# Moving the homes of TensorE's operands in SBUF by a few dozen bytes

## The chip, the cores and the metric

The kernel runs on one core of a Trainium2 chip. The metric is the time of one execution on the device in microseconds (us), as the median of several runs.

## What is computed

Attention with two kinds of window feeds a token mixer and a feed-forward block, all in fp32 (B = 8 sequences, H = 8 heads, S = 576, D = 64; model width 512, inner width 2048):

```python
scores = where(mask, q @ k.T / sqrt(64), -1e9)     # heads 0-3: band of 32; heads 4-7: every 4th of 128
x = softmax(scores) @ v                            # heads side by side: [8, 576, 512]
mixed = real(fft(fft(x, axis=1), axis=2))
u = x + mixed
un = (u - mean(u)) / sqrt(var(u) + 1e-6)           # over the 512 channels
out = u + maximum(un @ w_ch1, 0) @ w_ch2           # 512 -> 2048 -> 512
```

`w_ch1` and `w_ch2` arrive as 64-bit floats and are turned into fp32 on the chip.

## The kernel before

Each operation is handed to a planner (`Plan`) with its engine, an estimated cost, a priority and the buffers that it reads and writes. The planner simulates the engines and writes out one order of instructions per engine. Buffers with a tag share a fixed number of slots (`ut` 4, `h` 6, `row` 2); a tile's place in SBUF comes from the pool that it is taken from.

The work has three parts. Attention and the mix (Fourier transforms as matmuls against the tables `seq`, `chn`, `tail_sb`, `alt_sb`) run sequence by sequence in the first part. In the gaps, and behind them, the **filling stage** takes pairs of token tiles through the first NF1 = 5 of 16 slices of the inner width: `up` (L926) multiplies tokens `ut` by `wa1`, the relu's output goes to `h`, `down` (L942) multiplies `h` by `wa2`, and the sum over these five slices is put away in memory. The **second stage** takes 9 chunks of 512 tokens (4 token tiles of 128) through the other 11 slices: `product` (L1199) multiplies blocks of the first weight by `xb`, the tokens of the chunk in 7 combinations, and `down` (L942) the relu's output by `wd` and `wa2`. A chunk has passes p = 0 to 5. A pass of two slices has 7 products of 6 matmuls (42) and up to 8 downs of 3 matmuls (24, for the slices of the pass before); pass 5 has one slice and 24 product matmuls. Its blocks come from `ups`:

```python
ups = [
    [block(pair0, i) for i in range(7)],
    [block(pair1, i) for i in range(7)],
    [block(pair2, i) for i in range(5)] + [block(more, i) for i in range(2)],
    [block(tail_w, i) for i in range(4)] + [spare_up(i) for i in range(3)],   # spare_up: in wa1
    [spare_up(3 + i) for i in range(7)],
    [block(tail_w, 4 + i) for i in range(3)],
]
```

Every product in fp32r is three matmuls, high and low halves: (high, high), (low, high), (high, low). The two halves of a buffer lie whole multiples of 512 bytes apart, and so do the slices that a matmul takes. All of these matmuls load a new stationary operand of 128 columns. The moving operand has 256 columns in `up` and `product`, 512 in `down`. In `up` and `product` the weight is stationary and the tokens move; in `down` `h` is stationary and the weight moves.

SBUF is filled from two sides. On the left lie, in this order, the pool `ffn` (tags `ut`, `h`, `row`), `const` (`flip_sb`, `wa1`, `wa2`) and then `mix`, which `second()` closes and replaces by `pair1`, `more`, `wd2` to `wd5`, `xb` and the buffers `s1` to `c22`. On the right lies `att`, which `first()` closes and replaces by `pair0`, `wd0`, `wd1`, `pair2` and the staging buffers, these later by `tail_w` (`third()`). [...] The start of each buffer in a partition, modulo 128, is in the program:

| buffer | start modulo 128, before |
|---|---|
| `ut`, `h`, `row` | 0 |
| `wa1`, `wa2`, `pair1`, `more`, `wd2` to `wd5`, `xb` | 32 |
| `pair0`, `wd0`, `wd1`, `pair2`, `tail_w` | 96 |
| `tq`, `kb`, `pm`, `perm_sb` (attention) | 64 |
| `ident_sb`, `ptsb` | 32 |

In what follows, two operands of a matmul are called n apart when their starts modulo 128 differ by n, counted the shorter way.

Of the kernel before, what the change touches and what calls it, by code (L numbers as in the profile page):

```python
# [9 lines left out]
F32 = mybir.dt.float32  # L10
F32R = mybir.dt.float32r
I32 = mybir.dt.int32
# [7 lines left out]
P = 128  # L20
# [5 lines left out]
TOK1 = 2 * P  # L26
# [6 lines left out]
NH = 6  # L33
# [144 lines left out]
class Plan:  # L178
# [20 lines left out]
    def add(self, eng, cost, fn, r=(), w=(), prio=0.0, nbytes=0, at=0.0):  # L199
        op = Op()  # L200
        op.eng, op.cost, op.fn, op.prio, op.nbytes = eng, cost, fn, prio, nbytes
        op.num, op.after, op.ready, op.start = len(self.ops), [], at, None
        self.ops.append(op)
        deps, bufs = set(), {}
        for items, writes in ((r, False), (w, True)):
            for it in items:
                b, key = it if isinstance(it, tuple) else (it, None)
                bufs[id(b)] = b
                keys = set(b.writer) | set(b.readers) if key is None else {key, None}
                for x in keys:  # L210
                    if x in b.writer:
                        deps.add(b.writer[x])
                    if writes:
                        deps.update(b.readers.get(x, ()))
        for items, writes in ((r, False), (w, True)):
            for it in items:
                b, key = it if isinstance(it, tuple) else (it, None)
                if writes:
                    if key is None:
                        b.writer, b.readers = {None: op.num}, {}  # L220
                    else:
                        b.writer[key] = op.num
                        b.readers.pop(key, None)
                else:
                    b.readers.setdefault(key, []).append(op.num)
        op.bufs = list(bufs.values())
        for b in op.bufs:
            b.left += 1
        deps.discard(op.num)
        op.waits = len(deps)  # L230
        for d in deps:
            self.ops[d].after.append(op)
        return op
# [134 lines left out]
def fused_kernel(ctx: ExitStack, tc, q, k, v, w1, w2, seq, tail, chn, alt, mask, ident, perm, flip, out):  # L368
    nc = tc.nc
    plan = Plan()  # L370
# [11 lines left out]

    pools = {}
    pools["psum"] = ctx.enter_context(tc.tile_pool(name="psum", bufs=1, space=bass.MemoryType.PSUM))
    pools["ffn"] = ctx.enter_context(tc.tile_pool(name="ffn", bufs=1))
    const = ctx.enter_context(tc.tile_pool(name="const", bufs=1))
    mix_ctx, att_ctx, stage_ctx = ExitStack(), ExitStack(), ExitStack()
    pools["mix"] = keep = mix_ctx.enter_context(tc.tile_pool(name="mix", bufs=1))
    pools["att"] = heads = att_ctx.enter_context(tc.tile_pool(name="att", bufs=1, side="right"))

# [3 lines left out]
    def bank(tag):  # L394
        return plan.buf(lambda: pools["psum"], tag, [P, 512], F32, banks[tag])
# [9 lines left out]
    def ffnb(tag, shape, dtype=F32, bufs=2):  # L405
        return plan.buf(lambda: pools["ffn"], tag, shape, dtype, bufs)

    def fixed(pool_, shape, dtype, name):
        b = Buf(ap=pool_.tile(shape, dtype, name=name))
        if pool_ is keep:  # L410
            mixed.add(id(b))
        return b

    def utb(i=0):
        return ffnb("ut", [P, 2, KT, TOK1], F32R, NUT)

    flip_sb = fixed(const, [P, 8], I32, "flip_sb")
    wa1 = [fixed(const, [P, 2, KT, P], F32R, f"wa1_{f}") for f in range(NF1)]
    wa2 = [fixed(const, [P, 2, C], F32R, f"wa2_{f}") for f in range(NF1)]
    mask_sb = fixed(heads, [QB, 3, KB], F32, "mask_sb")  # L420
# [15 lines left out]
    def dma(fn, r, w, prio, nbytes, slow=1):  # L436
        return add("SP", 0.5, fn, r, w, prio, nbytes * slow)
# [3 lines left out]
    def start():  # L441
        dma(lambda: nc.sync.dma_start(out=mask_sb(), in_=mask), (), (mask_sb,), -7.9, QB * 3 * KB * 4)
        dma(lambda: nc.sync.dma_start(out=ident_sb(), in_=ident), (), (ident_sb,), -7.8, P * 3 * P * 4)
        dma(lambda: nc.sync.dma_start(out=perm_sb(), in_=perm), (), (perm_sb,), -7, QB * QB * 12)
        dma(lambda: nc.sync.dma_start(out=flip_sb(), in_=flip), (), (flip_sb,), 50, P * 32)

        def zero(t, eng, cost, fn, key=None, prio=-5.0):
            add(eng, cost, fn, (), ((t, key) if key is not None else t,), prio)

        zero(half, "DVE", 0.07, lambda: nc.vector.memset(half(), -0.5))  # L450
        for n, t in enumerate(kbs):
            for e in range(2):
                def clear(t=t, e=e):
                    ps = slice(64 * e, 64 * e + 64)
                    nc.vector.memset(t()[ps, 1 - e], 0.0)
                    nc.vector.memset(t()[ps, e, 0:WIN], 0.0)
                zero(t, "DVE", 0.8, clear, ("z", e), -6.0 + n)
        for t in xs + xtail:
            zero(t, "DVE", 0.07, lambda t=t: nc.vector.memset(t()[:, C:C + 1], 0.0), "pad")
        def gaps():  # L460
            for r in (32, 96):
                nc.vector.memset(eot().bitcast(F32)[r:r + 32, 0], 0.0)
        zero(eot, "DVE", 0.4, gaps, ("gap", 0))
        zero(eot, "DVE", 0.2, lambda: nc.vector.memset(eot().bitcast(F32)[0:32, 1], 0.0), ("gap", 1))
        zero(ye, "DVE", 0.2, lambda: nc.vector.memset(ye().bitcast(F32), 0.0))
        for b in range(B):
            dma(lambda b=b: nc.sync.dma_start(
                out=xsm[b]()[0:1], in_=kbs[0]()[0:1, 1, WIN:WIN + C],
            ), ((kbs[0], ("z", 0)),), ((xsm[b], "zero"),), 12 * b + 6, 2048)
        for i in range(2):  # L470
            for m in range(2):
                add("POOL", 0.06, lambda i=i, m=m: nc.gpsimd.dma_start(out=seq_sb[i]()[:, m], in_=seq[i, m]),
                    (), ((seq_sb[i], m),), 6 + i, P * 2 * NSP * 4, at=T_SEQ + i)
                add("POOL", 0.06, lambda i=i, m=m: nc.gpsimd.dma_start(out=chn_sb[i]()[:, m], in_=chn[i, m]),
                    (), ((chn_sb[i], m),), 9 + i, P * 2 * NEP * 4, at=T_CHN + i)
        add("POOL", 0.06, lambda: nc.gpsimd.dma_start(out=tail_sb(), in_=tail), (), (tail_sb,), 6.5, P * 3 * NSP * 4, at=T_SEQ + 0.5)
        add("POOL", 0.06, lambda: nc.gpsimd.dma_start(out=alt_sb(), in_=alt), (), (alt_sb,), 8, P * NEP * 4, at=T_SEQ + 4)
# [461 lines left out]
    def down(h, wf, acc, s, first, last, prio):  # L939
        def go():  # L940
            for n, (a, p) in enumerate(PASSES):
                nc.tensor.matmul(  # L942
                    acc(), lhsT=h()[:, a, P * s:P * s + P], rhs=wf()[:, p],
                    start=(first and n == 0), stop=(last and n == 2),
                )
        add("PE", 3 * pe(C), go, (h, wf), (acc,), prio)
# [140 lines left out]
    def fill(ut, tiles, at=None):  # L1087
        prio = P_FILL + (tiles[0] if at is None else at) * P_FILLT
        late = at == NREST - 1 or tiles[0] < NREST <= tiles[0] + 2 * NLATE
        hs = []  # L1090
        for f in range(NF1):
            h = ffnb("h", [P, 2, TOK1], F32R, NH)
            z = bank(("pt", "av")[f % 2] if late else "ff")
            hs.append(up(ut, wa1[f], z, h, prio, TOK1))
        for s, idx in enumerate(tiles):
            acc = bank("sc" if late else "ff")
            for f in range(NF1):
                down(hs[f], wa2[f], acc, s, f == 0, f == NF1 - 1, prio)
            keep_part(idx, acc, prio)
# [20 lines left out]
    def second():  # L1120
        mix_ctx.close()
        pools["wbb"] = left = ctx.enter_context(tc.tile_pool(name="wbb", bufs=1))
        pair1.ap = tile_of(left, 7, "pair1")
        more.ap = tile_of(left, 2, "more")
        for i in range(2, 6):
            wd[i].ap = left.tile([P, 2, C], F32R, name=f"wd{i}")
        xb.ap = left.tile([P, 7, 2, 2, TOK1], F32R, name="xb")

    def third():
# [86 lines left out]
        return s  # L1216

    def put_h(z, need):
        h = ffnb("h", [P, 2, TOK1], F32R, NH)
        add("ACT", act(TOK1), lambda: nc.scalar.activation(  # L1220
            out=h()[:, 0], in_=z(), func=AF.Relu), need, ((h, 0),), SOON)
        add("DVE", dve(TOK1), lambda: nc.vector.scalar_tensor_tensor(
            h()[:, 1], z(), 0.0, h()[:, 0].bitcast(F32), op0=ALU.max, op1=ALU.subtract),
            (*need, (h, 0)), ((h, 1),), SOON)
        return h
# [89 lines left out]
```

## Time and profile before

| | |
|---|---|
| median of 3 runs | 1122.07 us (1121.26 to 1122.24) |
| the profiled execution | 1123.04 us |
| its span, first to last instruction | 1121.3 us |
| mean granted TensorE clock | 0.981 |
| TensorE matmuls busy | 1072.7 us, 96% of the span, 7066 matmuls |
| VectorE busy | 726.6 us, 65% |
| ScalarE busy | 522.5 us, 47% |
| GpSimd busy | 289.4 us, 26% |

"Busy" is the time in which an engine has at least one instruction under way. Matmuls overlap, so their own durations (some 280 ns for 256 columns, 395 ns for 512) are longer than the interval from one start to the next. The chain of work follows the last instruction back to what released it; its pieces join without gaps, so a piece of n matmuls divided by n gives their interval.

### The profile page before, as it was taken

Reading aid. Unit: us, or ns where it says so; the run is one execution under the profiler, and the core shown is the slowest. Engines: PE = TensorE matmul, PEld = TensorE weight load, DVE = VectorE, ACT = ScalarE, POOL = GpSimd, SP = SyncE. Lnnn points to the kernel's source line nnn. Section 1 sums busy time; section 2 is a strip of 40 time slices with the busy share of each in tenths; the row PEclk is TensorE's granted clock in tenths of the full one; section 3 lists DMA queues with packets and bytes.
Section 4 is the critical chain, followed back from the end, with each engine's and each line's share of the span. In section 5 each row is a group of like instructions: output and inputs, shape, how many; then the busy total and the mean of one; then the engine's idle time right before and its main releaser. Section 6 shows DMA issues by size and latency. Waiting matters only on the chain.

```text
span 1121.3 us, 20217 instructions
## 1 busy us (share of the span) xinstructions
PE 1072.7 (96%) x7066; PEld 948.1 (85%) x7066; DVE 726.6 (65%) x2318; ACT 522.5 (47%) x1331; POOL 289.4 (26%) x341
## 2 busy tenths in 40 slices
PE   5799999999999999999989899999999999999997
PEld 3567888889888988899978798898988889888886
DVE  5789988767867778867769763536363545454523
ACT  4587656546555634344435443333333333333331
POOL 2025365343434254300030421121202120212200
PEclk8799999999999999999999899999999999999999
DMA  9677567656655344345423250505050504041211
GB/s 313 175 207 220 159 193 195 193 143 184 176 165 149 115 136 123 110 122 152 129 87 114 66 160 1 150 1 151 1 150 1 142 9 132 20 107 45 93 59 38
DMA packets 104310, 137.05 MB, mean 122 GB/s; under 512 B 9656, under 2 KB 62328, under 8 KB 104208
## 3 DMA queue, kind: packets, MB, share of 16 engines
q1 hardware_dynamic: 100624, 126.85, 39.0%
q0 software_dynamic: 3040, 8.09, 2.4%
q8 instruction: 56, 0.92, 0.3%
q10 hardware_dynamic: 544, 0.82, 0.2%
q14 instruction: 46, 0.38, 0.1%
HBM read 97.92 MB, written 37.80 MB: 121 GB/s over the span
## 4 chain that ended last, share of the span: by engine, by line
PE 81%; DVE 11%; DMA 3%; issue 2%; POOL 1%; ACT 1%; SPq 0%; DVEq 0%; ACTq 0%; POOLq 0%
PE sc L942 15%; PE ff L1199 13%; PE mix L1199 8%; PE ff L926 7%; PE pt L942 6%; PE av L942 6%; PE ff L942 6%; PE sc L513 5%; PE av L547 5%; PE mix L775 2%; PE pt L540 2%; PE mix L729 2%; PE pt L926 2%; DVE pm L521 2%; DMA ut<-in_w_dram 1%
## 5 line engine op out<-in xcount | busy, mean ns | idle before, releaser
L527 ACT ACTIVATE pm<-pm,mx 96x128 f32<-96x128 f32 x384 | 130.3, 394 | 53.6 <-DVE mx L521 49.9
L1215 ACT COPY s<-ff 128x256 f32<-128x256 f32 x135 | 50.2, 373 | 163.9 <-PE ff L1199 163.5
L513 PE MATMUL sc<-kb,tq 128*96 128x256 f32 x384 | 109.4, 405 | 16.2 <-DMA kb<-in_k_dram 8.0
L926 PE MATMUL ff<-ut,wa 128*128 128x256 f32 x780 | 110.0, 291 | 3.3 <-DVE h L934 3.3
L521 DVE CUSTOM_DVE_ANT_0 pm<-sc,mask_sb 96x128 f32<-96x128 f32 x384 | 92.8, 278 | 24.4 <-PE sc L513 23.4
L942 PE MATMUL sc<-wa,h 128*128 128x512 f32 x420 | 106.4, 395 | 0.0
L926 PEld LDWEIGHTS ff<-ut,wa 128*128 128x128 f32 x780 | 99.7, 192 | 5.1 <-DVE h L934 3.9
L942 PE MATMUL ff<-wa,h 128*128 128x512 f32 x390 | 95.8, 397 | 0.0
L547 PEld LDWEIGHTS av<-vt,ptsb 128*96 128x96 f32 x768 | 79.9, 171 | 16.7 <-issue 5.5
L1068 POOL TENSOR_TENSOR ut<-ut 128x512 f32<-128x512 f32 x36 | 50.7, 1428 | 166.5 <-DVE ut L1024 86.4
L547 PE MATMUL av<-vt,ptsb 128*96 128x65 f32 x768 | 84.5, 253 | 6.9 <-DVE xt L559 5.3
L942 PEld LDWEIGHTS sc<-wa,h 128*128 128x128 f32 x420 | 76.2, 188 | 15.6
L942 PEld LDWEIGHTS ff<-wa,h 128*128 128x128 f32 x390 | 71.6, 188 | 15.7
L942 PE MATMUL sc<-wd,h 128*128 128x512 f32 x324 | 84.1, 394 | 0.0
L513 PEld LDWEIGHTS sc<-kb,tq 128*96 128x96 f32 x384 | 57.9, 173 | 30.0 <-issue 13.3
L1246 DVE TENSOR_TENSOR c<-s,s 128x256 f32<-128x256 f32 x45 | 22.3, 496 | 89.6 <-ACT s L1215 86.5
L1199 PEld LDWEIGHTS ff<-xb,pair 128*128 128x128 f32 x540 | 74.0, 189 | 6.6 <-ACT s L1215 0.7
L1024 DVE STREAM_TRANSPOSE ut<-ut 128x512 f32<-128x512 f32 (+1 forms) x76 | 71.7, 984 | 11.0 <-DMA ut<-us 10.9
L1199 PE MATMUL ff<-xb,pair 128*128 128x256 f32 x540 | 76.8, 281 | 0.5 <-ACT s L1215 0.5
L1081 POOL TENSOR_TENSOR xb<-ut,xb 128x512 fp32r<-128x512 f32 x27 | 36.8, 1363 | 133.5 <-ACT xb L1078 133.5
L1220 ACT ACTIVATE h<-row 128x256 fp32r<-128x256 f32 x90 | 37.5, 417 | 64.1 <-DVE row L1236 38.2
L980 POOL DMA_INDIRECT ut<-us,flip_sb x20 | 19.8, 988 | 180.9 <-DMA ut<-us 87.2
(158 smaller groups left out, 2318.4 us busy)
## 6 DMA issues: line engine op xcount, KB each, us to landing
vt<-in_v_dram SPq DMA_DIRECT2D x32, 390.0 KB
ut<-in_w_dram SPq DMA_DIRECT2D x20, 512.0 KB
us<-uc SPq DMA_DIRECT2D x36, 257.0 KB
tq<-in_q_dram SPq DMA_DIRECT2D x32, 288.0 KB
part<-row SPq DMA_DIRECT2D x36, 256.0 KB
ut<-us SPq DMA_DIRECT2D x36, 256.0 KB
ut<-part SPq DMA_DIRECT2D x36, 256.0 KB
kb<-in_k_dram SPq DMA_DIRECT2D x62, 144.0 KB
```

Source lines behind the costliest of these rows:

```text
L513: nc.tensor.matmul(sc()[:QB, 256 * n:256 * n + 256], lhsT=tq()[:, cols], rhs=kb()[:, :, keys], start=True, stop=True,)
L521: nc.vector.tensor_tensor_reduce(pm()[:, i], sc()[:QB, KB * i:KB * i + KB], mask_sb()[:, masks[blocks[i // 2]]], -0.125, 3.0e38, ALU.add, ...
L527: add("ACT", 0.295, lambda i=i: nc.scalar.activation(out=pm()[:, i], in_=pm()[:, i], func=AF.Exp, bias=mx()[:, i:i + 1], scale=-1.0), ((mx ...
L547: add("PE", 0.16, lambda i=i: nc.tensor.matmul(av()[:QB, 65 * i:65 * i + 65], lhsT=pt()[:, i], rhs=vt()[:, i % 2, blocks[i // 2]], start=T ...
L926: nc.tensor.matmul(z()[:, :n_tok], lhsT=wf()[:, a, kk], rhs=ut()[:, p, kk], start=(kk == 0 and n == 0), stop=(kk == KT - 1 and n == 2),)
L942: nc.tensor.matmul(acc(), lhsT=h()[:, a, P * s:P * s + P], rhs=wf()[:, p], start=(first and n == 0), stop=(last and n == 2),)
L1024: nc.vector.transpose(out=o[back], in_=x[:, g])
L1068: add("POOL", pool(C), lambda: nc.gpsimd.tensor_tensor(out=made(i)(), in0=x(), in1=y(), op=ALU.subtract), (*done, *((raw, ("s", j)) for j ...
L1081: add(eng, (pool if eng == "POOL" else dve)(C), lambda j=j, get=get, lo=lo: lo.tensor_tensor(out=xb()[:, j, 1], in0=get(), in1=xb()[:, j, ...
L1199: nc.tensor.matmul(z()[:, lo:lo + TOK1], lhsT=ap()[:, a, kk], rhs=xb()[:, j, p, kk], start=(start and k == 0), stop=(stop and k == 6 * len ...
L1215: add("ACT", act(TOK1), lambda: nc.scalar.copy(out=s(), in_=src()[:, :TOK1]), (src,), (s,), SOON - 1)
L1220: add("ACT", act(TOK1), lambda: nc.scalar.activation(out=h()[:, 0], in_=z(), func=AF.Relu), need, ((h, 0),), SOON)
```

## The change: other homes for buffers

Nothing but the place of tiles in SBUF is changed. `flip_sb` gets a pool of its own at the left edge, 64 bytes wide, so that `ut` and `row` behind it start at 64. `h` leaves the pool `ffn` for a pool `hidden` behind a gap of 64 bytes, and starts at 0, as do `wa1` and `wa2` behind it. On the right, 96 unused bytes bring `pair0`, `wd0`, `wd1`, `pair2` and `tail_w` from 96 to 0. In `second()`, `pair1`, `more` and `wd2` to `wd5` come to lie at 0 by the 96 bytes gained on the left, and 64 unused bytes put `xb` at 64. Everything on the right moves by 96 bytes, attention's buffers too (64 becomes 96), and so does the mix's part of the left (`ident_sb`: 32 becomes 0).

| matmul | stationary, moving before | apart | after | apart |
|---|---|---|---|---|
| `up` | `wa1` 32, `ut` 0 | 32 | 0, 64 | 64 |
| `down` with `wa2`, `wd2` to `wd5` | `h` 0, weight 32 | 32 | 0, 0 | 0 |
| `down` with `wd0`, `wd1` | `h` 0, weight 96 | 32 | 0, 0 | 0 |
| `product` with `pair1`, `more`, `wa1` | 32, `xb` 32 | 0 | 0, 64 | 64 |
| `product` with `pair0`, `pair2`, `tail_w` | 96, `xb` 32 | 64 | 0, 64 | 64 |

```diff
     pools["psum"] = ctx.enter_context(tc.tile_pool(name="psum", bufs=1, space=bass.MemoryType.PSUM))
+    index = ctx.enter_context(tc.tile_pool(name="index", bufs=1))
+    flip_sb = Buf(ap=index.tile([P, 16], I32, name="flip_sb"))
     pools["ffn"] = ctx.enter_context(tc.tile_pool(name="ffn", bufs=1))
+    gap = ctx.enter_context(tc.tile_pool(name="gap", bufs=1))
+    gap.tile([P, 16], F32, name="gap")
+    pools["hidden"] = ctx.enter_context(tc.tile_pool(name="hidden", bufs=1))
     const = ctx.enter_context(tc.tile_pool(name="const", bufs=1))
     mix_ctx, att_ctx, stage_ctx = ExitStack(), ExitStack(), ExitStack()
+    side = ctx.enter_context(tc.tile_pool(name="side", bufs=1, side="right"))
+    side.tile([P, 24], F32, name="side")
...
+    def hidden():
+        return plan.buf(lambda: pools["hidden"], "h", [P, 2, TOK1], F32R, NH)
+
...
-    flip_sb = fixed(const, [P, 8], I32, "flip_sb")
...
-        dma(lambda: nc.sync.dma_start(out=flip_sb(), in_=flip), (), (flip_sb,), 50, P * 32)
+        dma(lambda: nc.sync.dma_start(out=flip_sb()[:, 0:8], in_=flip), (), (flip_sb,), 50, P * 32)
...
-            h = ffnb("h", [P, 2, TOK1], F32R, NH)
+            h = hidden()
...
             wd[i].ap = left.tile([P, 2, C], F32R, name=f"wd{i}")
+        left.tile([P, 16], F32, name="step")
         xb.ap = left.tile([P, 7, 2, 2, TOK1], F32R, name="xb")
...
-        h = ffnb("h", [P, 2, TOK1], F32R, NH)
+        h = hidden()
```

## Rows read from the trace of the kernel before

**Rows 1.** The page: span, busy time of each engine, chain by engine.
```profile
span 1121.3 us, 20217 instructions
...
PE 1072.7 (96%) x7066; PEld 948.1 (85%) x7066; DVE 726.6 (65%) x2318; ACT 522.5 (47%) x1331; POOL 289.4 (26%) x341
...
PE 81%; DVE 11%; DMA 3%; issue 2%; POOL 1%; ACT 1%; SPq 0%; DVEq 0%; ACTq 0%; POOLq 0%
```

**Rows 2.** Waits of TensorE, 585 to 1121 us: total, times, longest.
```profile
PE ff L1199 <- ACT h L1220: 3.0, 1, 3.0
PE ff L1199 <- ACT s L1215: 0.5, 1, 0.5
```

**Rows 3.** Stretches: busy us of each engine, granted clock, DMA share, GB/s.
```profile
300.00:400.00 100.00, 99.98 (x736) 88.83 (x735) 73.21 (x352) 57.90 (x161) 35.91 (x53) 1.00 0.51 148
...
703.00:761.00 58.00, 58.00 (x366) 52.13 (x365) 28.71 (x53) 22.27 (x53) 11.11 (x9) 1.00 0.26 71
```

**Rows 4.** The chain, 540 to 645 us: start, us, what.
```profile
565.37 1.68 DVE xb L1081
567.04 1.68 DVE ut L860
...
625.88 2.00 DVE ut L1024 x2
```

**Rows 5.** The chain, one chunk of the second stage, 703 to 761 us.
```profile
706.92 0.69 PE ff L1199 x6
...
711.85 1.44 PE mix L1199 x12
713.28 1.40 PE sc L942 x6
...
721.72 0.69 PE ff L1199 x6
722.41 1.36 PE mix L1199 x12
...
732.19 0.69 PE ff L1199 x6
...
742.71 0.71 PE ff L1199 x6
743.42 1.44 PE mix L1199 x12
...
753.28 1.41 PE ff L1199 x12
...
756.10 1.37 PE ff L1199 x12
```

**Rows 6.** The chain, filling stage, 464 to 499 us: `down` x30, `up` x60 and x36.
```profile
470.36 7.00 PE ff L942 x30
477.36 7.10 PE ff L926 x60
484.46 6.99 PE ff L942 x30
491.44 4.26 PE ff L926 x36
```

**Rows 7.** Stretches, instructions of L926 alone: busy us of matmuls and loads.
```profile
300.00:400.00 100.00, 26.76 (x180) 23.28 (x180) 1.00 0.51 148
400.00:580.00 180.00, 85.22 (x660) 83.33 (x660) 0.98 0.43 128
```

**Rows 8.** Groups by line and shape: the transposes in attention (busy, mean ns).
```profile
L540 PE MATMUL pt<-ident_sb,pm 96*128 96x96 f32 x192 | 32.1, 260 | 1.0 <-ACT ptsb L543 1.0
...
L540 PE MATMUL pt<-perm_sb,pm 96*128 96x96 f32 x192 | 30.8, 254 | 3.3 <-ACT ptsb L543 2.4 <-ACT pm L527 0.6
```

## Prediction

> **What bounds the kernel now.** I read the page first, then the chain of work, then the waits, then single stretches of the chain. The page's head and shares [rows 1] say that TensorE is busy for 96% of the span and holds 81% of the chain. The reader should see that this leaves little else to gain from, but also that "busy" tells nothing of pace: a matmul that takes longer is just as busy. So the second question is who TensorE waits for. [...] Only around 427 to 464, 556 to 570 and 622 to 636 us does the chain run mostly over VectorE; three of its pieces are shown [rows 4].
>
> The third look is at pace. In the chain, pieces of one line follow each other without a gap, so a piece's time divided by its count is the interval of a matmul. Rows 5 hold pieces of one chunk, all of them the same instruction: 128 stationary columns, 256 moving ones, the same clock. The products with pair1 (711.85) and with wa1 (743.42) take 1.44 us for 12, which is 120.0 ns. Those with pair2 (722.41) and tail_w (753.28, 756.10) take 1.36, 1.41 and 1.37, which is 113.3, 117.5 and 114.2 ns. By homes, the first two weights start 32 bytes past a multiple of 128, and so does xb: the two operands are 0 apart modulo 128. The others start at 96: they are 64 apart from xb. The matmuls of `up` in the filling stage (weights at 32, tokens at 0, so 32 apart) take 7.10 us for 60 and 4.26 for 36, 118.3 ns [rows 6]. `down` streams 512 columns with h at 0 against weights at 32 or 96, 32 apart either way; 30 take 7.00 or 6.99 us [rows 6] and six of the second stage take 1.40 [rows 5], 233 ns in each.
>
> Whole stretches of one chunk confirm it. From the starts at 721.72, 732.19, 742.71 and 753.28 [rows 5], passes p = 2, 3 and 4 take 10.47, 10.52 and 10.57 us for the same 42 products and 24 downs. They hold 12, 18 and 42 products that are 0 apart. So 30 more of these cost 0.10 us, 3.3 ns each.
>
> **The change part by part.** Every instruction, its order, its waits and the DMAs stay: the planner sees the same tags, slots and costs. Homes alone move. Four families of matmuls get another distance between stationary and moving operand.
>
> A. Products with pair1, more and wa1: 0 apart becomes 64 apart. Per chunk these are 42 (p = 1), 12 (p = 2), 18 (p = 3) and 42 (p = 4), 114; in 9 chunks 1026. At 3.3 ns each: 3.4 us saved. The ends come from rows 5: down from 120.0 to 117.5, 2.6 us; down to 113.8 (the mean of 1.36 and 1.37 over 12), 6.4 us. Nothing saved stays as an end too, if the distance is not the cause (below).
>
> B. `up` in the filling stage: 32 apart becomes 64. It has 1080 matmuls, of which 180 and 660 start after 300 us [rows 7], where TensorE sets the pace; the 240 before I count at nothing, since VectorE, ScalarE and DMA share the chain there. 64 apart costs, as the mean of today's mix, 120.0 - 3.3 = 116.7 ns; from 118.3 that is 1.6 ns times 840, 1.4 us saved. Ends: 117.5 ns, 0.7 us; 113.8 ns, 3.8 us.
>
> C. `down`, 1728 matmuls (540 in the filling stage, 1188 behind): 32 apart becomes 0 apart. No row shows 512 moving columns at 0. Nearest from above: 256 columns at 0 take 1.7 ns more than at 32 (120.0 against 118.3); so much on each of 1728 is 2.9 us lost, and if 512 columns cost twice 120.0, 240 ns, the loss is 6.7 ns each, 11.6 us. Nearest from below: twice 113.8 is 227.6, a gain of 5.7 ns each, 9.8 us. I take nothing: against weights at 32 and at 96, on either side of h, `down` shows the same 233 ns, so it is so far the family that homes move least. Both ends stay for the range.
>
> D. Products with pair0, pair2 and tail_w stay 64 apart, at 0 and 64 now and not at 96 and 32. Today 42 of 120 in a chunk run at the short pace (0.69 for 6 at 706.92, 721.72 and 732.19, 1.36 and 1.37 for 12 [rows 5]), the rest near 117.5. I take no change. All long would lose 42 x 9 x 3.7 ns = 1.4 us, all short gain 78 x 9 x 3.7 = 2.6 us.
>
> E. Attention's and the mix's operands move too, but all tiles of the right side move by the same 96 bytes, and those of the left side likewise, so their distances stay, with one exception: the transposes against ident_sb. They average 260 ns at 32 apart, those against perm_sb at 0 apart 254 [rows 8]; 6 ns on 192 is 1.2 us either way, and I take nothing.
>
> F. Writes by DMA and by the other engines go to other homes. DMA engines are 0.26 busy in a chunk and VectorE 28.71 of 58.00 us [rows 3]; that slack is the cover, and from 585 us on TensorE waited for no DMA at all [rows 2]. Without the cover, VectorE's stretch of 622 to 636 us would grow; ten per cent of it is 1.4 us.
>
> What is late next: where TensorE gets ahead, VectorE's two pieces at 565 and 567 us [rows 4] are met sooner, and a part of B can be lost there; B's lower end covers it.
>
> Sum: -3.4 - 1.4 = -4.8 us. The profiled execution took 1123.04 us (span 1121.3 [rows 1]), 0.97 above the median of the runs, 1122.07. It would take 1118.2, and the median becomes 1117.3.
>
> [...] The row shows 120.0 ns at 0 apart and 113.3 to 117.5 at 64 apart for one instruction at one clock [rows 5]. [...]
>
> **The rivals.** *All short.* Products 64 apart run at two paces that persist over a block, 113.8 and 117.5 ns. If aligned homes make the short one the rule, A gives 6.4, B 3.8 and D 2.6 us: 12.8, so 1109.3. For it: a block keeps its pace once it has it (12 in 1.36). Against it: today each chunk shows both, at one and the same distance.
>
> *All long.* The other pace everywhere: A 2.6 and B 0.7 saved, D 1.4 lost: 1.9, so 1120.2, not to be told from no change. For it: 78 of 120 run so today.
>
> *Homes are not the cause.* The weights that run at 120.0 ns also lie in the left part of the memory, as xb does, and the faster ones on the right. Then the region decides, the low bits do nothing, A and B are 0: 1122.1. For it: in this trace the two can't be told apart. Against it: `up` has both operands on the left and runs at 118.3, between the two.
>
> *Slower.* `down` at 0 apart pays as the products do. At 240 ns for 512 columns it loses 11.6 us against the 4.8 saved: +6.8, so 1128.9. It decides from 2.8 ns a matmul on (4.8 us over 1728). For it: 0 is the slowest distance that the rows show. Against it: a weight load is equally long in both families, and `down` runs twice as many moving columns beside it.
>
> **How the numbers follow.** 0.2% of the time, 2.2 us, is about what a measurement of this kernel can tell from no change. Forecast 0.42 (its own range 1113 to 1119.8), all short or a gain in `down` beside it 0.20, all long 0.10, homes not the cause 0.12, slower by `down` 0.16. Faster is the forecast, all short and a little of all long, 0.64; same 0.21; slower 0.15. The range takes the likeliest, the two that end near today, all short down to 1106, and the small losses in `down` up to 1124.5; it leaves out most of the slower case and a tail with `down` at 227.6.
>
> **What would show it.** In a chunk, pass p = 4 should fall from 10.57 towards 10.43 us, and 12 products with wa1 from 1.44 to 1.41 or less. 60 of `up` should fall from 7.10 to about 7.00. Thirty of `down` should stay within 6.95 to 7.05; 7.2 there would mean the slower case, 6.8 a gain that I have not counted. TensorE's granted clock and its waits should stay. The forecast is wrong if pass p = 4 keeps its 10.57 us, or if `down` moves by more than 2 ns.

## The result, and the profile after

The kernel after takes 1113.39 us (median of 6 runs, 1111.84 to 1114.71), the kernel before on the same chip 1122.63 (6 runs, 1121.26 to 1123.67). The ratio is 0.9917, interval 0.9904 to 0.993: 9.2 us faster. The profiled execution took 1114.71 us, 8.33 less than that of before.

The page of after, beside [rows 1]: span, busy time of each engine, chain by engine.

```profile
span 1112.9 us, 20217 instructions
...
PE 1064.3 (96%) x7066; PEld 944.7 (85%) x7066; DVE 726.0 (65%) x2318; ACT 522.2 (47%) x1331; POOL 288.7 (26%) x341
...
PE 80%; DVE 12%; DMA 3%; issue 2%; POOL 1%; ACT 1%; SPq 0%; DVEq 0%; ACTq 0%; POOLq 0%
```

TensorE executes the same 7066 matmuls and is busy 8.4 us less; the span is 8.4 us shorter. VectorE, ScalarE and GpSimd change by 0.7 us at most. The waits of TensorE from 580 us on, beside [rows 2], and two stretches, beside [rows 3]:

```profile
PE ff L1209 <- ACT h L1230: 3.1, 1, 3.1
PE ff L1209 <- ACT s L1225: 0.5, 1, 0.5
```

```profile
300.00:400.00 100.00, 99.98 (x739) 89.16 (x738) 73.51 (x352) 58.97 (x164) 36.25 (x53) 1.00 0.51 146
698.00:756.00 58.00, 58.00 (x368) 52.30 (x368) 28.68 (x53) 22.24 (x53) 11.14 (x9) 1.00 0.28 74
```

The waits are the old ones, within 0.1 us; the granted clock is 1.00 in both stretches, as before; TensorE is idle for 0.02 of these 158 us, before and after. So the gain is in the pace of its matmuls. It shows in the chain. First the filling stage (start, us, what), beside [rows 6]; L951 is `down`, L935 `up`:

```profile
468.68 6.81 PE ff L951 x30
475.50 7.07 PE ff L935 x60
482.56 6.80 PE ff L951 x30
```

Thirty of `down` took 7.00 and 6.99 us and take 6.81 and 6.80: 233 ns became 227. Sixty of `up` went from 7.10 to 7.07, a mere 0.5 ns each. Then a chunk of the second stage, beside [rows 5]; L1209 is `product`:

```profile
706.87 1.36 PE mix L1209 x12
...
716.65 0.69 PE ff L1209 x6
...
727.04 0.72 PE ff L1209 x6
...
737.47 0.71 PE ff L1209 x6
738.18 1.41 PE mix L1209 x12
739.59 1.39 PE sc L951 x6
...
747.97 1.37 PE ff L1209 x12
```

Products with wa1 (738.18) take 1.41 us for 12 where they took 1.44; those with pair1 (706.87), 1.36. The starts 716.65, 727.04, 737.47 and 747.97 give passes p = 2, 3 and 4: 10.39, 10.43 and 10.50 us, before 10.47, 10.52 and 10.57. Six of `down`, however, take 1.39 here (739.59), little less than the 1.40 of before, at the same distance at which thirty in a row of the filling stage went to 227 ns. Over the whole second stage these downs gain more than this one piece shows (a table by family stands below).

Where the time came from can be read off without the chain. The order of the 7066 matmuls is the same in all kernels below, so the start of the n-th, counted from 0, is a waypoint (us from the span's start; the 3600th lies near the end of the filling stage, and from the 4200th to the 7000th TensorE never stops: 445.00 of the 445.00 us from 655 to 1100 are busy, before and after). Starts by the trace:

```
matmul         500th     3600th    4200th    7000th    4200th to 7000th
before         100.47    548.79    655.07    1101.36   446.29
after          101.07    545.91    650.54    1093.19   442.65
```

From the 500th to the 3600th 3.5 us are gained, to the 4200th another 1.6, from there to the 7000th 3.6.

### The profile page after: what moved, and what is told of

It is laid out like the page before. It is cut to its first block, busy times and chain, and to the rows that moved or that the text cites. A ratio compares the mean times of both kernels' runs of the same rounds, so it can differ in the third digit from the quotient of the medians.

```text
span 1112.9 us, 20217 instructions
## 1 busy us (share of the span) xinstructions
PE 1064.3 (96%) x7066; PEld 944.7 (85%) x7066; DVE 726.0 (65%) x2318; ACT 522.2 (47%) x1331; POOL 288.7 (26%) x341
## 4 chain that ended last, share of the span: by engine, by line
PE 80%; DVE 12%; DMA 3%; issue 2%; POOL 1%; ACT 1%; SPq 0%; DVEq 0%; ACTq 0%; POOLq 0%
PE sc L951 14%; PE ff L1209 13%; PE mix L1209 8%; PE ff L951 6%; PE ff L935 6%; PE pt L951 6%; PE av L951 6%; PE sc L522 6%; PE av L556 4%; PE mix L784 2%; PE mix L738 2%; PE pt L549 2%; PE pt L935 2%; DVE pm L530 1%; DMA ut<-in_w_dram 1%
## 5 line engine op out<-in xcount | busy, mean ns | idle before, releaser
L935 PE MATMUL ff<-ut,wa 128*128 128x256 f32 x780 | 109.0, 289 | 3.7 <-DVE h L943 3.6
L951 PE MATMUL sc<-wa,h 128*128 128x512 f32 x420 | 104.4, 391 | 0.0
L935 PEld LDWEIGHTS ff<-ut,wa 128*128 128x128 f32 x780 | 98.7, 192 | 5.7 <-DVE h L943 4.3
L951 PE MATMUL ff<-wa,h 128*128 128x512 f32 x390 | 93.8, 392 | 0.0
L951 PEld LDWEIGHTS sc<-wa,h 128*128 128x128 f32 x420 | 76.0, 188 | 13.8
L951 PE MATMUL sc<-wd,h 128*128 128x512 f32 x324 | 83.7, 393 | 0.0
L951 PEld LDWEIGHTS ff<-wa,h 128*128 128x128 f32 x390 | 71.6, 188 | 13.8
L1209 PEld LDWEIGHTS ff<-xb,pair 128*128 128x128 f32 x540 | 73.8, 188 | 6.4 <-ACT s L1225 0.7
L1209 PE MATMUL ff<-xb,pair 128*128 128x256 f32 x540 | 76.4, 280 | 0.5 <-ACT s L1225 0.5
```

The source lines that it names most:

```text
L935: nc.tensor.matmul(z()[:, :n_tok], lhsT=wf()[:, a, kk], rhs=ut()[:, p, kk], start=(kk == 0 and n == 0), stop=(kk == KT - 1 and n == 2),)
L951: nc.tensor.matmul(acc(), lhsT=h()[:, a, P * s:P * s + P], rhs=wf()[:, p], start=(first and n == 0), stop=(last and n == 2),)
L1209: nc.tensor.matmul(z()[:, lo:lo + TOK1], lhsT=ap()[:, a, kk], rhs=xb()[:, j, p, kk], start=(start and k == 0), stop=(stop and k == 6 * len ...
```

## The experiments

**Homes modulo 256.** The prediction took distances modulo 128. The runs below showed that the period is 256 (e6), so distances are given here as start of the moving minus start of the stationary operand, modulo 256:

| distance modulo 256 of | before | after |
|---|---|---|
| `up` | 224 | 192 |
| `down` with `wa2`, `wd2` to `wd5` | 32 | 0 |
| `down` with `wd0`, `wd1` | 96 | 128 |
| `product` with `wa1`, `pair1`, `more` | 0 | 64 |
| `product` with `pair0`, `pair2`, `tail_w` | 192 | 192 |

**One part alone: e1, e11, e7.** e1 is the kernel before with `h` alone moved, by 32 bytes modulo 256 (part C): `row` and `flip_sb` stand before it and not behind it. `wa2` and `wd2` to `wd5` are then 0 from it, `wd0` and `wd1` 64.

```diff
+    index = ctx.enter_context(tc.tile_pool(name="index", bufs=1))
+    flip_sb = Buf(ap=index.tile([P, 8], I32, name="flip_sb"))
+    pools["hidden"] = ctx.enter_context(tc.tile_pool(name="hidden", bufs=1))
...
-            h = ffnb("h", [P, 2, TOK1], F32R, NH)
+            h = hidden()
```

> The kernel before with h alone moved, from 0 to 32, so that down has its operands 0 apart and all else stays. Theory 1, the distance between the two operands of a matmul modulo 128 sets its pace: thirty downs of the filling stage take 6.8 us in place of 7.0, and the time falls by some 6 us to about 1116.5. Rival, absolute alignment counts (starts at multiples of 64 are read faster): h gets worse, down stays at 233 ns or slower, and the time is 1122.6 or above.

Measured: 1118.04 us, before 1122.56; ratio 0.9959 (0.9943 to 0.9974). The chain of e1 in the filling stage (L947 `down`, L931 `up`):

```profile
465.70 6.83 PE ff L947 x30
472.52 7.10 PE ff L931 x60
```

`down` fell to 227.7 ns, `up` kept its 7.10. Moving one buffer inside the same region does this, and to a start of 32 modulo 128, which is less aligned than the 0 of before. Nor is it the place of `h` as such: in e11 below `h` lies at the very bytes of after, 32 from `wa2`, and thirty take 7.00. Neither the region nor the alignment of an operand is the cause here; the distance of the two is.

e11 gives `up` alone its distance of after, 192 (part B): the weights, `h` and `xb` all move by 128 bytes modulo 256, `ut` by 96, so that all other distances of the table stay.

```diff
+    lead = ctx.enter_context(tc.tile_pool(name="lead", bufs=1))
+    lead.tile([P, 24], F32, name="lead")
     pools["ffn"] = ctx.enter_context(tc.tile_pool(name="ffn", bufs=1))
+    gap = ctx.enter_context(tc.tile_pool(name="gap", bufs=1))
+    gap.tile([P, 8], F32, name="gap")
+    pools["hidden"] = ctx.enter_context(tc.tile_pool(name="hidden", bufs=1))
...
         pair2.ap = tile_of(right, 5, "pair2")
+        right.tile([P, 32], F32, name="side")
```

> The kernel before with the tokens of the filling stage alone moved against wa1: ut 64 bytes off it (192 modulo 256, as in the kernel after), products and down keep their distances modulo 256. The prediction's part B alone: 1.4 us saved, 1121.2; by the intervals of the kernel after (116.3 ns against 118.3 on 840 matmuls that TensorE sets the pace of) 1.7 us, 1120.9. Rival, the gain is lost at VectorE's stretches: 1122.6.

Measured: 1120.58, before 1123.08; ratio 0.9976 (0.9967 to 0.9986). Chain (L950 `down`, L934 `up`):

```profile
467.53 7.00 PE ff L950 x30
474.53 7.07 PE ff L934 x60
```

e7 is the kernel before with `xb` 64 behind the blocks on the left, and the blocks on the right moved so that they too are 64 from it and no more 192. So it is part A with D at 64, and it takes `wd0` and `wd1` from 96 to 32 from `h`:

```diff
         pair2.ap = tile_of(right, 5, "pair2")
+        right.tile([P, 16], F32, name="side")
...
+        left.tile([P, 16], F32, name="step")
         xb.ap = left.tile([P, 7, 2, 2, TOK1], F32R, name="xb")
```

> The kernel before with the second stage's tokens alone moved against the blocks: xb at 96, all blocks at 32, so 64 apart everywhere; up and down keep their 32 apart. The prediction's part A alone: 3.4 us saved, 1119.2. By what the kernel after showed of the products (253.3 us against 255.2 in all) it is 2 us, 1120.6, since blocks that ran at the short pace lose it behind another entry.

Measured: 1120.91, before 1122.59; ratio 0.9984 (0.9974 to 0.9993). Its chain, passes p = 2 to 4:

```profile
720.06 0.71 PE ff L1201 x6
...
730.58 0.71 PE ff L1201 x6
...
741.10 0.71 PE ff L1201 x6
...
751.62 1.42 PE ff L1201 x12
```

Each pass takes 10.52 us: p = 4 has gained 0.05, p = 3 nothing, and p = 2, whose pair2 blocks ran at 1.36 before, has lost 0.05. The twelve that open pass 5 take 1.42 (751.62). So 64 apart ran at some 118 ns throughout these passes (1.42 over 12), and not at the mean of the mix of before.

These medians must not be added up as they stand. They hold the first part too, where the granted clock differs between executions. Two stretches, 449 to 517 us of before and of e7:

```profile
449.00:517.00 68.00, 65.53 (x406) 58.96 (x405) 50.04 (x110) 26.25 (x58) 10.89 (x14) 0.97 0.40 121
```

```profile
449.00:517.00 68.00, 65.38 (x408) 58.26 (x408) 51.38 (x110) 26.40 (x58) 10.46 (x14) 1.00 0.41 124
```

No matmul in there has an operand that e7 moves, yet between the 3000th and the 3400th (449.22 to 516.67 us of before) e7 gains 1.03 us, at a clock of 1.00 instead of 0.97. In e1 and e11 it is 1.00 there too, in after 0.97. So the parts are compared from the 4200th matmul to the 7000th, where the clock is the same (1.00 from 655 to 1100 us in each of the kernels below; 2800 matmuls at 366 a chunk, 7.65 of the 9 chunks):

```
4200th to 7000th, us                                    against before
before                                        446.29
e11  up alone                                 446.29     0.00
e7   products all 64 apart                    445.92    -0.37
e1   h moved, products as before              445.82    -0.47
e5   blocks at 16                             447.39    +1.10
e9   as after, products all 64 apart          444.40    -1.89
e2   as after, h 64 from wa2                  443.69    -2.60
after                                         442.65    -3.64
e3   as after, all homes 32 further           442.65    -3.64
e8   tokens 112 from all blocks               437.98    -8.31
```

e7 and e1 give 0.37 and 0.47, together (e9, where the downs with wd0 and wd1 are 0 apart too) 1.89, and with pair0, pair2 and tail_w at 192 (after) 3.64. The effects of two families that take turns don't add. The reason shows when the same 2800 intervals, each from the start of a matmul to the next start, are summed by family (us against before):

```
                                                after      e1      e7      e9
C   down with wa2, wd2 to wd5           x822    -1.84   -1.51   -0.59   -2.07
    down with wd0, wd1                  x192    -0.01   +0.10   -0.27   -0.55
A   products with pair1, more, wa1      x892    -1.19   +0.35   -0.77   -0.62
D   products with pair0, pair2, tail_w  x894    -0.60   +0.60   +1.26   +1.36
```

Where two families meet, an interval could as well be counted to the matmul that follows; this shifts single sums by up to 0.6 us and leaves every sign. In e1 `down` gains 1.51 us, but the products, none of which moved against `xb`, lose 0.95 (0.31 by the other count). In e7 the moved products of A gain 0.77, those of D lose 1.26 by going from 192 to 64, and `down` with `wa2` and `wd2` to `wd5` gains 0.59 although it did not move. So a family's pace depends on the distances of its neighbours too, and e7's total is not the worth of A.

**Other distances for `h`, and all homes 32 further: e2, e3.** Both are the kernel after. e2 puts the gap of 64 bytes behind `h`, which is then 64 from `wa2`; e3 makes the index tile 32 bytes wider on the left and the side tile 32 narrower on the right.

```diff
-    gap = ctx.enter_context(tc.tile_pool(name="gap", bufs=1))
-    gap.tile([P, 16], F32, name="gap")
     pools["hidden"] = ctx.enter_context(tc.tile_pool(name="hidden", bufs=1))
+    gap = ctx.enter_context(tc.tile_pool(name="gap", bufs=1))
+    gap.tile([P, 16], F32, name="gap")
```

> The kernel after with h alone moved, from 0 to 64, so that down is 64 apart; up and product stay 64 apart. Theory 1: down loses what 0 apart gave it, 233 ns again, and the time is about 1119.5, 6 us above the kernel after. Rival, absolute alignment: h is still at a multiple of 64, down stays at 227 to 230 ns, and the time stays 1113.4.

Measured: 1114.97, before 1122.56; ratio 0.9939 (0.9926 to 0.9952), 1.6 above after.

```diff
-    flip_sb = Buf(ap=index.tile([P, 16], I32, name="flip_sb"))
+    flip_sb = Buf(ap=index.tile([P, 24], I32, name="flip_sb"))
...
-    side.tile([P, 24], F32, name="side")
+    side.tile([P, 16], F32, name="side")
```

> The kernel after with every home 32 bytes higher: weights and h at 32, tokens at 96, all distances as after, no start at a multiple of 64. Theory 1: 1113.4 as after, thirty downs in 6.8 us. Rival, absolute alignment: the gain goes, 1122.6.

Measured: 1113.7, before 1122.56; ratio 0.9922 (0.9908 to 0.9935). The chains of e2, then of e3:

```profile
467.51 6.87 PE ff L951 x30
474.37 6.83 PE ff L935 x60
```

```profile
467.77 6.81 PE ff L951 x30
474.59 7.07 PE ff L935 x60
```

e3 runs at the pace of after to the digit, at starts that are no multiples of 64: for this kernel, moved by 32 bytes as a whole, the distances are all there is. e2 missed, and by itself it would fit the rival of alignment: it is e1 and e3 that rule this out. 64 apart is good for `down` as well, 229 ns, and `up`, whose homes are those of after, ran at 113.8 ns beside it, where after has 117.8.

**All distances, by themselves: e4.** Matmuls alone; attention, mix and feed-forward are left out. Rows of 36 at the distances 0, 16, ... 112 (da to dh), rising from start 0, then falling from start 32, with 512 columns and then 256.

```python
for k in range(COUNT):
    a, p = ((0, 0), (1, 0), (0, 1))[k % 3]
    s, m = base + 128 * a, base + d + n * p
    nc.tensor.matmul(z[:, :n], lhsT=stat[:, s:s + 128], rhs=mov[:, m:m + n],
                     start=(k == 0), stop=(k == COUNT - 1))
```

> Matmuls alone (attention, mix and feed-forward are left out): 36 in a row with a load of 128 stationary columns each, for distances 0, 16, 32, to 112 between the operands (bank da to dh), first with 512 moving columns and then with 256, each from a start at 0 (distances rising) and at 32 (distances falling). Theory 1: the interval depends on the distance and not on the start: with 512 columns 227 ns at 0 and 233 at 32 and 96; with 256 columns 120 at 0 behind other blocks, 118 at 32, 113 or 118 at 64. Rival, absolute alignment: the two starts differ at the same distance by 3 ns or more.

The chain of e4; a piece divided by its count is the interval. The first two are 512 columns, the rest 256:

```profile
23.74 8.40 PE dc L33 x36
...
40.54 8.25 PE de L33 x36
...
148.95 4.20 PE dc L33 x36
...
157.41 4.24 PE de L33 x36
...
165.97 4.32 PE dg L33 x36
170.28 8.20 PE dh L33 x72
```

With 512 columns: 233.3 ns at 32, 229.2 at 64. With 256: 116.7 at 32, 117.8 at 64, 120.0 at 96, and 113.9 at 112 (dh, both rows in one piece). The rows from start 32 agree with those from start 0 within 0.04 us, but for 256 columns at 16 (4.21 against 4.28 us) and 512 at 48 (8.28 against 8.39). So the best distance for 256 columns is not the best for 512.

**Finer steps, the period, and turns: e6.** Matmuls alone again: turns of 6 with 256 and 6 with 512 columns, then rows of 36 with 256 columns at 96 to 124 in steps of 4, at 112, 240, 368, 496, at 64, 192, 320, 448, and with 512 columns at 0, 128, 256, 384.

```diff
+    for i, (d, e) in enumerate(PAIRS):
+        for _ in range(REPS):
+            block(small[i % 4], d, 256, 6)
+            block(large[i % 4], e, 512, 6)
```

> Matmuls alone again (the rest is left out). First eight pairs of distances, moving past stationary, for 256 and 512 columns in turns of six and six as in the second stage, twelve turns each: (0, 32), (64, 32), (64, 0), (112, 0), (112, 64), (112, 112), (112, 32), (112, 16). If each kind kept the pace of long rows, a turn would take 2120, 2106, 2066, 2040, 2053, 2068, 2080 and 2070 ns. Rival, entry decides: turns with 0 for 512 columns take 2080 or more, as in the kernel after. Then 36 of 256 columns at 96 to 124 in steps of 4, to see how wide the good place at 112 is, then at 112, 240, 368, 496 and 64, 192, 320, 448, and 36 of 512 columns at 0, 128, 256, 384: if the period is 128 bytes, the four of a kind agree.

Its chain: 256 columns at 108, 112 and 116, then at 240 and 368, then 512 columns at 0, 128 and 256.

```profile
222.48 4.30 PE pd L36 x36
226.78 4.12 PE pa L36 x36
230.90 4.38 PE pb L36 x36
...
248.08 4.22 PE pb L36 x36
252.30 4.13 PE pc L36 x36
...
277.62 8.16 PE qa L36 x36
285.78 8.39 PE qb L36 x36
294.17 8.18 PE qc L36 x36
```

112 is short (4.12), 108 and 116 are not (4.30, 4.38). 368 is short as 112 is, 240 is not (4.22, and 496 the same); with 512 columns 0 and 256 take 226.7 and 227.2 ns, 128 and 384 take 233.1 and 233.6. So over the distances tried, 0 to 496, a period of 256 bytes fits and one of 128 does not. In turns, 64 apart (256 columns) with 0 apart (512) takes 2.09 us, near what after shows (0.71 and 1.39), where the paces of long rows would give 2.07; 112 for both takes 2.07.

**Blocks off a multiple of 32: e5.** The kernel before with the blocks of the first weight 16 bytes past a multiple of 128 and everything else at 0, so that they are 112 apart from the tokens modulo 128.

```diff
-        return pool_.tile([P, n, 2, 2, P], F32R, name=name)
+        t = pool_.tile([P, n * C + 32], F32R, name=name)
+        return t[:, 4:4 + n * C].rearrange("p (n a k f) -> p n a k f", n=n, a=2, k=2)
```

> The first weight's blocks (wa1, pair0 to pair2, more, tail_w) 16 bytes past a multiple of 128, tokens, h and the second weight at 0. Tokens then lie 112 past the blocks, the distance that took 113.3 ns from either side in the row of matmuls alone; down stays 0 apart. If distance in these low bits is all, products and up run at 113.3 to 114 ns nearly everywhere: 2106 products save some 3 ns and 1080 ups some 2.5 ns against the kernel after, 8 us in all, so about 1105. Rival, that a block of six has no time to settle and its pace is that of its entry: products stay at 116 to 118 ns and the time stays near 1113.

Measured: 1123.5, before 1122.59; ratio 1.0011 (1.0002 to 1.0019). The forecast gain did not come. Twelve products with wa1 took what they did before, and thirty of `down` 6.97:

```profile
742.92 1.44 PE mix L1203 x12
```

One reason is the period (modulo 256 `h` and `wa2` came to lie 128 apart, not 0, 233.1 ns for 226.7 in e6, and the blocks on the right 240 from the tokens, not 112, 117.2 ns for 114.4); the other is e10.

**Starts and history: e10.** Matmuls alone: rows of 36 at 64 (pa) and 112 (pb) with the stationary operand at 0, 16, 32, 48, 128 and 144, then 64 and 192 by turns (`qa` between them: 512 columns at 0).

```diff
+BASES = (0, 16, 32, 48, 128, 144)
...
+    for base in BASES:
+        for i, d in enumerate((64, 112)):
+            block(small[i], base, d, 256, COUNT)
...
+    for i, d in enumerate((64, 192, 64, 192, 64)):
+        block(small[i % 2], 0, d, 256, COUNT)
```

> Matmuls alone (the rest is left out), 36 in a row, stationary starts at 0, 16, 32, 48, 128 and 144. With 256 columns at distances 64 and 112 in turns: if distance alone counts, 117.8 and 113.3 ns from every start; if a stationary start off a multiple of 32 spoils it, 112 takes some 120 ns from 16, 48 and 144 (which would tell why the blocks at 16 lost). With 512 columns at 0: 226.7 from every start. Then 256 columns at 64, 192, 64, 192, 64: 117.8 in each if they are one place, as in the earlier row; 113.3 behind a change if the change itself starts the short pace. Last, six at 192, twelve at 64, six of 512 columns at 0, in turns: the twelve at 113.3 if so.

Its chain: pb (112 apart) from starts 0, 16 and 32; then 192 (pb) and 64 (pa) by turns.

```profile
13.46 4.08 PE pb L36 x36
...
21.80 4.31 PE pb L36 x36
...
30.35 4.14 PE pb L36 x36
...
113.66 4.09 PE pb L36 x36
117.74 4.24 PE pa L36 x36
```

112 apart takes 113.3 ns from start 0, 115.0 from 32, and 119.7 from 16, where e5 had put its blocks. 512 columns at 0 (`qa`) took 227.1 to 227.9 ns from starts 0, 32 and 128 and 230 from 16, 48 and 144, by the starts in the trace. And 192 apart took 113.6 ns here, but 117.8 in e6: the same instruction at the same homes, in both cases behind a row at 64. The last part, turns of 6 at 192, 12 at 64 and 6 of 512 columns, did not give the short pace that was expected for the twelve (1.41 or 1.42 in every turn).

**All blocks on one side of the period: e9, e8.** e9 is after with the blocks on the right at multiples of 256, so that all products are 64 apart, as in e7, and all downs 0 apart. Attention's buffers on the right go back by 96 bytes with them.

```diff
-    side = ctx.enter_context(tc.tile_pool(name="side", bufs=1, side="right"))
-    side.tile([P, 24], F32, name="side")
...
         pair2.ap = tile_of(right, 5, "pair2")
+        right.tile([P, 56], F32, name="side")
```

> The kernel after with the blocks on the right at multiples of 256 and not 128 past them, so that wd0 and wd1 are 0 apart from h modulo 256 and not 128. If the period for 512 columns is 256 bytes, the downs of pass p = 1 gain up to 4 ns each, 1 us in all: 1112.4. If it is 128, no change from 1113.4.

Measured: 1117.3, before 1122.67; ratio 0.995 (0.9937 to 0.9963): 4 us slower than after, where a gain was expected; 1.75 us of it lie between the 4200th and the 7000th matmul. The downs with wd0 and wd1 gained 0.54 us there against after, in the direction forecast (0 apart modulo 256 and not 128), but with pair2 at 64 and not 192, the short pace is gone:

```profile
719.08 1.41 PE mix L1208 x12
```

e8 takes e9 and puts the tokens, and `wd0` to `wd5`, 112 past a multiple of 256.

```diff
+        t = left.tile([P, 7 * 4 * TOK1 + 64], F32R, name="xb")
+        xb.ap = t[:, 28:28 + 7 * 4 * TOK1].rearrange("p (j a k t) -> p j a k t", j=7, a=2, k=2)
```

> The kernel after with all weights' blocks at multiples of 256, and xb, wd0 to wd5 112 past them; h, wa2, ut as after. The pair (112, 112) took 2066 ns a turn among the turns alone, (64, 0) 2093. If the turns alone tell of the kernel, passes p = 1 to 3 fall by 0.1 us each and more, and the time by some 4 to 6 us below the kernel after, to 1107 to 1109. Rival, that it is the entry into each block and the kernel mixes blocks differently: products stay at 116 to 118 ns and the time stays at 1112 to 1115 or rises.

Measured: 1109.91 (1108.11 to 1113.5), before 1122.67; ratio 0.9894 (0.9878 to 0.991). It beats both kernels. Its chain, passes p = 2 and 3 (10.31 and 10.30 us from the starts at 715.83, 726.14 and 736.44):

```profile
715.83 0.68 PE ff L1212 x6
716.51 1.36 PE mix L1212 x12
717.87 1.39 PE sc L949 x6
...
726.14 0.68 PE ff L1212 x6
...
736.44 0.68 PE ff L1212 x6
```

All products of these passes are at the short pace, 0.68 for 6; `down` at 112 takes the 1.39 of after.

## Why the prediction was right in its sign and short in its size

**What bounds the kernel.** Right that pace is what was left to gain. Neither the waits (3.1 and 0.5 us, [rows 2] 3.0 and 0.5) nor the granted clock of the stretches (1.00) moved; TensorE's pace alone did, and the span followed it us for us (8.4 and 8.4). That the chain runs mostly over VectorE in no more than three stretches holds from 300 us on; before that it does so from 89.4 to 107.9 us too (13.4 of 18.5 us).

**The cause.** Right that homes set the pace, and by their distance, though the period is 256 bytes and not the 128 that the prediction took: e1, e3 and e11 show the first (thirty of `down` take 6.83, 6.81 and 7.00 us), e6 the second (226.7, 233.1 and 227.2 ns at 0, 128 and 256). In e1 one buffer moved, and the same 30 matmuls took 6.83 us where they took 7.00. The rival that homes or their low bits do nothing (1122.1) falls with it. What in the chip makes a distance dear no run shows.

**C, `down`, is the step that failed.** It was taken as nothing, since 32 apart on either side of `h` gave one pace. That was an argument from two places at one distance. It is the largest part, in both stages. In the filling stage thirty in a row went from 233.2 to 226.8 ns (7.00 and 6.81 us), and over all its 540, shorter rows included, the mean interval fell by 5.7 ns, 3.1 us. Rows of thirty went even past the lower end, 5.7 ns. In the second stage the same distances gave 1.84 us between the 4200th and the 7000th matmul, 2.2 over 9 chunks: less for each matmul (232.6 to 230.3 ns); six in a row between products did not reach the pace of thirty. I had named 6.8 us for 30 as the sign of a gain not counted, and a move of `down` by more than 2 ns as a sign that the forecast is wrong; both came (6.81 us, and 6 ns). The bound from above, and with it the slower case, rested on products being slow at 0: 512 columns are quickest where 256 are among the slowest (226.7 ns in e6, 120.0 in rows 5). The weight loads, which the case against it calls equally long, averaged 188 to 191 ns in `down` and 189 to 197 in `up` and `product` (groups by line and shape of before).

**A was forecast at 3.4 us and gave 1.4** (1.19 x 9 / 7.65). The 3.3 ns a product came from passes with different blocks, as if 64 apart had one mean. The three passes themselves did not fit one price: from p = 2 to 3 six more products cost 0.05 us, from 3 to 4 twenty-four more cost as much. 64 took 117.8 ns in long rows (e4, e6), 2.2 under 120.0, and the blocks of pair0, pair2 and tail_w, which modulo 128 looked the same, lie at 192 and can go short (113.6 in e10). So p = 4 fell to 10.50 and not to 10.43; 12 with wa1 fell to 1.41 as forecast.

**D was taken as nothing and gave 0.7** (0.60 x 9 / 7.65), though these blocks stay at 192: pair2 and tail_w ran short more often beside the moved families (intervals of 115 ns or less, by the starts in the trace: 122 of 240 became 211, and 97 of 360 became 200; of pair0 21 of 294 became 2). C, A and D together make the 4.3 us of the second stage (0.48 a chunk). Counted by the interval that ends at each matmul, C, A and D would be 2.3, 0.9 and 0.9.

**B was forecast at 1.4 us.** By pace it gives 0.03 us per 60 or 0.5 ns, on 840 matmuls 0.4 us, in after and in e11 alike. The 2.5 us of e11's median are more, and its clock of 1.00 in 449 to 517 us accounts for about 1; the rest is not settled.

**E and F were right.** The transposes against `ident_sb` and `perm_sb` average 263 and 255 ns in after (groups by line and shape), beside 260 and 254 [rows 8]; VectorE's stretch of 622.6 to 635.7 us took 13.1 us and takes 13.1 (619.3 to 632.4):

```profile
L549 PE MATMUL pt<-ident_sb,pm 96*128 96x96 f32 x192 | 32.5, 263 | 1.0 <-ACT ptsb L552 1.0
L549 PE MATMUL pt<-perm_sb,pm 96*128 96x96 f32 x192 | 31.0, 255 | 3.3 <-ACT ptsb L552 2.4 <-ACT pm L536 0.6
```

**The sum.** 3.1 (C, filling) + 0.4 (B) + 4.3 (second stage) = 7.8 of the 8.33 us between the two profiled executions; the rest is not assigned. The medians are 9.2 apart, and the difference is within their intervals. Forecast were 4.8, all of it in A and B, which gave 1.8; C gave 5.3. That the time still lies in the forecast's own range (1113 to 1119.8) is luck: two terms were too large and one that was left out made up for them. Of a gain in `down` the far end, 9.8 us, was named, but the range left it out, and the chances had it only beside all short, at 0.20. The rival "all short" named a time near that of e8, for another reason: not that homes are aligned, but that they lie 112 apart, where the short pace is the rule (0.68 for 6). "All long" is what e7 and e9 show for products at 64 (118.0 to 118.3 ns). Not settled is what decides between the two paces at 192, or at 64, where pair1 in after took 1.36 for 12; and how one family's distance changes the pace of the next.

## What to carry to other kernels

Where TensorE never waits, look at the interval from one matmul's start to the next in rows of one instruction; if it differs between buffers, compare their starts modulo 256 (the period in e6), moving against stationary. Try the distance for each shape in long rows, and then in the real alternation: here a gain of 0.19 us on thirty of `down` shrank to 0.01 on six, and moving `h` in e1 slowed products that did not move by 0.95 us (0.31 by the other count). A family seen at one distance only is not a family without effect: `down` took 233 ns at 32 and 227 at 0.

## What the runs showed of the hardware that was not expected

- Rows of 36 of one instruction (the first row of a program aside) took 113.3 to 121.9 ns a matmul with 256 moving columns and 226.7 to 233.6 ns with 512, by the distance of the two operands modulo 256 bytes (e4, e6, e10, with mean granted clocks over the whole run of 1.0, 0.96 and 0.931).
- For 256 columns the short pace at 112 is gone 4 bytes to either side (114.4 against 119.4 and 121.7 ns, e6), and gone if the stationary operand starts at 16 (119.7, e10). A start of 32 keeps most of it (115.0).
- At 192 apart one and the same row, behind a row at 64 both times, ran at 113.6 or 117.8 ns (e10, e6), and `up` at 192 ran at 113.8 ns with `down` at 64 (e2) and at 117.8 with `down` at 0 (after). That what ran before decides would fit both; no run here isolates it.
